# Inverse row sums brought to the features' partitions by one product with a 0/1 matrix of heads, in place of two transposes

## The chip, the core and the metric

The kernel runs on one core of a Trainium2 chip. A core has engines that run side by side, each through its own instructions in order: TensorE (PE, with its weight loads PEld), VectorE (DVE), ScalarE (ACT), GpSimd (POOL) and SyncE (SP), which issues most transfers. They wait for one another through semaphores. On-chip memory has 128 partitions; TensorE writes into PSUM, which the kernel uses in banks. The metric is the device time of one execution in microseconds.

## What is computed

Attention with a hash mask, then a feed-forward network (FFN) over all tokens. Cut to what matters, with 4 batches, 8 heads, 768 positions, head size 64, model width 512 and FFN width 2048:

```python
mask = q_bucket[:, :, :, None] == k_bucket[:, :, None, :]   # 6 sign bits of a projection
scores = np.where(mask, scale * q @ k.T, -1e9)
attn = np.exp(scores - scores.max(-1))
attn = attn / (attn.sum(-1) + 1e-09)
x = (attn @ v) with heads side by side: (3072 tokens, 512)
h = x @ w_in
out = (h * np.clip(h + 3, 0, 6) / 6) @ w_out
```

The division by the row sum belongs to a token and a head. The kernel does not divide the attention matrix. It multiplies the attention's output by 1 / (row sum + 1e-9) just before the FFN reads it.

## The kernel before

**Precision.** Operands of the large matmuls are split into a rounded high part and the rest (type fp32r), and three products, high x high, high x low and low x high, are added in PSUM. Splits are a copy on ACT for the high part and a subtraction on DVE or POOL for the low part.

**Attention.** A step k works on 128 queries of one head; 6 steps make a head and 192 make the whole. `scores` (L405) fills a pair of PSUM banks. `lowest` on DVE (L412) takes the row minimum of the negated scores and copies them to SBUF, and `exponential` on ACT (L424) gives the probabilities, with the row sums as a by-product in `sms[b]`, tokens on partitions: [128, 6, 8 heads]. Then the probabilities are turned so that keys are on partitions. Up to step 101 PE does this with transposes (`transp`, L434); later `flip` on DVE (L445) transposes blocks of 32x32, and `move` sends them through DRAM into the tiles `spare` and `px`. `split_p` (L491 on ACT, L493 on POOL, L495 on DVE) splits them, `values` (L517, L531) multiplies by v, `output` (L567) copies out of PSUM, and SP and POOL (`add`, L542) write the transposed result, unnormalised, to DRAM. Once per head the next head's hash bits are taken: `hash_qk` (L345) on PE and `bits` (L364) on DVE.

**FFN.** Batch 0 is done in the middle of the kernel by `first_ffn`. Batches 1 to 3 are done by the generator `ffn`, in chunks of 256 tokens, three to a batch, nine in all; chunks are named b_t for batch and chunk here. A chunk takes 16 steps, one for each 128 columns of the FFN's width: `gemm1` (L686, 12 matmuls of 256 columns), `gate` (L708 on ACT, L709 on DVE, then L714 on ACT and L715 on DVE for the split) and `gemm2` (L724, L725, L729) for the step before. The FFN generator is advanced by hand inside the attention's steps at the calls `go("A")` to `go("D")`, and the order of PE, DVE, ACT and POOL is written out by hand (`manual_schedule`). From step 101 on this is called paced. After the attention ends, the rest of the FFN runs alone; that stretch is the tail here.

**Normalising a chunk.** `load_x` brings the chunk's features back from DRAM as `xr`, [128 features, 4 groups, 256 tokens]. Features are on partitions, but the inverse row sums have tokens on partitions. `scale_x` lists six things to do, and `begin` puts them into `side`, from which the FFN's loop takes one at a time beside its own work (in paced steps for batches 1 and 2 one per step, in stage D at the step's end; for batch 3 two per step, after some empty entries):

1. `invert`: `inverse` on DVE, one addition (L587) and one reciprocal (L588) of 128x16;
2. `spread_next(0)`: `spread` on POOL (L597) copies the inverse of the group's two heads 64 times each into a tile of 128x256 behind the home in `spare`;
3. to 6., for each group of 128 features: `normalise` turns that tile with two transposes on PE (L607) into the PSUM tile `rt`, DVE multiplies the features by it (L610), and POOL spreads the next group, into the same tile.

The multiplications on DVE are collected in `muls` and issued by `multiply()`: in paced steps after the next exponential, and in held steps after the split of the probabilities. When the last step of a chunk is reached, `split_x` (L675 on ACT, L676 on DVE) splits the next chunk's features; for batch 3 this is done group by group.

Chunk 1_0 is normalised before pacing begins, at steps that are marked `held`. PSUM banks for `rt`, `h`, `z` and `acc` come from `bank`, four in turn.

Of the kernel before, what the change touches and what calls it, by code (L numbers as in the profile page):

```python
# [10 lines left out]
F32 = mybir.dt.float32  # L11
F32R = mybir.dt.float32r
BF16 = mybir.dt.bfloat16
U32 = mybir.dt.uint32
AF = mybir.ActivationFunctionType
ALU = mybir.AluOpType
AX = mybir.AxisListType

P = 128
# [24 lines left out]
def lsh_attention_moe(  # L44
# [10 lines left out]
    nc = tc.nc  # L55
    B, H, D, S = qkT.shape
    D //= 2
    DM, DF = w_in.shape
    KT = S // P
# [4 lines left out]
    TC = 256  # L64
# [4 lines left out]
    cp = ctx.enter_context(tc.tile_pool(name="cp", bufs=1))  # L69
    sp = ctx.enter_context(tc.tile_pool(name="sp", bufs=2))  # L70
# [12 lines left out]
    spare = []  # L83
# [7 lines left out]
    turn = 0  # L91

    def bank(shape, name: str, tag: str | None = None):

        nonlocal turn
        if tag is None:
            tag = ("pt", "pu")[turn % 2]
            turn += 1
        return ps.tile(shape, F32, name=name, tag=tag, bufs=2)

    pair_turn = 0
    ffn_on = False
# [9 lines left out]
    thr = cp.tile([P, 1], F32, name="thr")  # L112
    val = cp.tile([P, 1], F32, name="val")
    three = cp.tile([P, 1], F32, name="three")
    ident = cp.tile([P, P], F32, name="ident")
    make_identity(nc, ident)


# [9 lines left out]
    for r, one, big in ((D, 0, -BIG), (ZK, 1, 1.0)):  # L128
# [3 lines left out]
        nc.vector.memset(val[r : r + 2 * NB], big * (1, -1)[1 - one])  # L132
        nc.vector.memset(val[r : r + NB], big * (1, -1)[one])
    nc.vector.memset(three[:], 3.0)

    raw0 = sp.tile([P, S], F32, name="raw0", tag="raw", bufs=1)[:]
    dma(out=raw0, in_=qkT[0, 0])
# [17 lines left out]
    WC = 512  # L155
# [70 lines left out]
    sms = {}  # L226
# [354 lines left out]
    def inverse(name: str, b: int, ts: slice, ccs: range, rc=None):  # L581

        k = slice(ts.start // P, ts.stop // P)
        hs = slice(ccs.start * P // D, ccs.stop * P // D)
        if rc is None:
            rc = sp.tile([P, KT, H], F32, name=f"rc{name}", tag="rc", bufs=1)[:, : k.stop - k.start]
        nc.vector.tensor_scalar_add(rc[:, :, hs], sms[b][:, k, hs], 1e-9)  # L587
        nc.vector.reciprocal(rc[:, :, hs], rc[:, :, hs])  # L588
        return rc

    def spread(name: str, rc, cc: int, to=None):

        hp2 = P // D
        rb = (spare[0][:, S : S + TC] if to is None else to).rearrange(
            "p (u h d) -> p u h d", u=TC // P, h=hp2
        )
        nc.gpsimd.tensor_copy(  # L597
            rb,
            rc[:, :, cc * hp2 : (cc + 1) * hp2].unsqueeze(3).to_broadcast([P, TC // P, hp2, D]),
        )  # L600
        return rb

    def normalise(name: str, x, rb, tag: str | None = None):

        rt = bank([P, TC], f"rt{name}", tag)
        for u in range(TC // P):
            nc.tensor.transpose(  # L607
                rt[:, u * P : (u + 1) * P], rb[:, u].rearrange("p h d -> p (h d)"), ident[:]
            )
        muls.append(lambda: nc.vector.tensor_mul(x, x, rt[:]))  # L610
        if not paced and not held:
            multiply()

    muls = []
    held = False

    def multiply():
        for f in muls:
            f()
        muls.clear()  # L620
# [3 lines left out]
    def piece():  # L624
        if pieces:
            pieces.pop(0)()

    def load_x(b: int, t: int, ccs: range, xr=None):
        assert not pending(b, range(ccs.start * P // D, ccs.stop * P // D), t)
        ts = slice(t * TC, (t + 1) * TC)  # L630
        if xr is None:
            xr = wide_tile([P, NCC, TC], F32, f"xr{b}_{t}")
        of = xs[b][:, ts].rearrange("(cc p) t -> p cc t", p=P)

        def load(cc: int):
            with tc.issue_after(last.ins):
                dma(out=xr[:, cc], in_=of[:, cc])

        if paced:
            for cc in ccs:  # L640
                pieces.append(lambda cc=cc: load(cc))
            piece()
        else:
            dma(out=xr[:, ccs.start : ccs.stop], in_=of[:, ccs.start : ccs.stop])
        return xr

    def scale_x(b: int, t: int, ccs: range, xr, rc=None):

        name = f"{b}_{t}"
        rbs = {}  # L650

        def invert():
            piece()
            def now():
                rbs["rc"] = rc if rc is not None else inverse(name, b, slice(t * TC, (t + 1) * TC), ccs)

            if held:
                muls.append(now)
            else:
                now()  # L660

        def spread_next(cc: int):
            piece()
            if cc < len(ccs):
                rbs[cc] = spread(name, rbs["rc"], cc)

        def then(cc: int):
            normalise(f"{name}_{cc}", xr[:, cc], rbs.pop(cc), "pt" if ffn_on and b == 0 else None)
            spread_next(cc + 1)

        return [invert, lambda: spread_next(0)] + [lambda cc=cc: then(cc) for cc in ccs]

    def split_x(x, src, engine):
        multiply()
# [117 lines left out]
    def widen(cc: int):  # L792

        hs = slice(cc * P // D, (cc + 1) * P // D)
        nc.scalar.copy(
            over[cc].rearrange("p (k h d) -> p k h d", k=KT, h=P // D),
            rc0[0][:, :, hs].unsqueeze(3).to_broadcast([P, KT, P // D, D]),
        )

    def divide(t: int, cc: int, tag: str | None = None):  # L800
        rb = over[cc][:, t * TC : (t + 1) * TC].rearrange("p (u h d) -> p u h d", u=TC // P, h=P // D)
        normalise(f"0_{t}_{cc}", xr0[t][:, cc], rb, tag)
# [5 lines left out]
    def late_rb():  # L808
        late["rc"] = inverse("late", 0, slice(0, S), range(cc3, NCC), rc0[0])
        x = sp.tile([P, NTC, TC], F32, name="rblate", tag="ga", bufs=1)  # L810
        late["rb"] = [
            spread(f"late{t}", late["rc"][:, 2 * t : 2 * t + 2], cc3, x[:, t]) for t in range(NTC)
        ]
# [49 lines left out]
    def first_ffn(resume):  # L863
        nonlocal ffn_on
        ffn_on = True
        normalise("late0", lt(0), late["rb"][0], "pt")
        split_x(x0[0][cc3], lt(0), nc.vector)
        room12(0)
# [74 lines left out]
        ffn_on = False  # L943
        yield

    first_x = []

    def load_first_x():
        spare.append(sp.tile([P, 2 * WC], F32, name="spare", tag="ob", bufs=1))
        first_x.append(load_x(1, 0, range(cc3)))  # L950

    def ffn():
# [10 lines left out]
        def begin(c: int):  # L963
            b, t = chunks[c]
            xr[c] = load_x(b, t, range(NCC) if c else range(cc3, NCC), None if c else first_x[0])
            todo = scale_x(b, t, range(NCC), xr[c])
            if b < B - 1:
                side.extend(todo + [lambda: None] * (0 if paced else 2))
                if not paced:
                    opening.append(lambda: (place(c), [split(c, cc) for cc in range(NCC)]))  # L970
                return

            side.extend([lambda: None] * (4 if t else 6) + todo[:2])
            for cc in range(NCC):
                side.append(todo[2 + cc])
                side.append(lambda cc=cc: (place(c) if cc == 0 else None, split(c, cc)))
# [161 lines left out]
    with tc.manual_schedule(engines={ET.PE, ET.DVE, ET.Activation, ET.Pool}):  # L1138
# [102 lines left out]
        for k in range(NS + LT + 2):  # L1241
# [4 lines left out]
            i, t = divmod(k, KT)  # L1246
# [4 lines left out]
            if k == GF - 6:  # L1251
                load_first_x()
# [123 lines left out]
```

## Time and profile before

| | |
|---|---|
| median of 3 runs | 962.6 us (962.13 to 962.63) |
| profiled execution, its own time | 964.03 us |
| its span, first to last instruction | 962.2 us |
| granted TensorE clock, mean | 1.000 |
| chunks' inversions (L587), start | 376.8, 440.2, 513.0, 584.9, 658.0, 730.4, 804.5, 850.7, 896.3 us |
| DMA | 152.06 MB, mean 158 GB/s |

The page's second part cuts the span into 40 equal slices of 24 us; each digit is the share in tenths that an engine was busy:

```profile
PE   8999999999999999999999999999999999999997
...
DVE  7999988888559999887878888877878874343422
ACT  7898875665469888667766766666766664333332
POOL 6777744666537766555655555555555442000000
```

The profile lists instructions by line of the kernel and engine. "p<-s" means that tile p is written from tile s. A bracket behind a row gives the time in which the engine stood idle before it, and whose work ended that wait. Idle time matters only on the path that sets the end. PE's matmuls overlap, so the distance between starts, not the duration, says what one costs PE.

### The profile page before, as it was taken

Reading aid. Unit: us, or ns where it says so; the run is one execution under the profiler, and the core shown is the slowest. Engines: PE = TensorE matmul, PEld = TensorE weight load, DVE = VectorE, ACT = ScalarE, POOL = GpSimd, SP = SyncE. Lnnn points to the kernel's source line nnn. Section 1 sums busy time; section 2 is a strip of 40 time slices with the busy share of each in tenths; the row PEclk is TensorE's granted clock in tenths of the full one; section 3 lists DMA queues with packets and bytes.
Section 4 is the critical chain, followed back from the end, with each engine's and each line's share of the span. In section 5 each row is a group of like instructions: output and inputs, shape, how many; then the busy total and the mean of one; then the engine's idle time right before and its main releaser. Section 6 shows DMA issues by size and latency. Waiting matters only on the chain.

```text
span 962.2 us, 19452 instructions
## 1 busy us (share of the span) xinstructions
PE 945.7 (98%) x6308; PEld 871.7 (91%) x6308; DVE 722.0 (75%) x1464; ACT 623.5 (65%) x1422; POOL 473.5 (49%) x584
## 2 busy tenths in 40 slices
PE   8999999999999999999999999999999999999997
PEld 7999988999989999889899999999899899899996
DVE  7999988888559999887878888877878874343422
ACT  7898875665469888667766766666766664333332
POOL 6777744666537766555655555555555442000000
PEclk9999999999999999999999999999999999999999
DMA  4567579100035455688888888788888773101000
GB/s 127 137 157 186 132 226 377 62 2 1 6 117 119 112 134 126 174 254 242 249 252 251 239 245 261 237 252 246 263 244 245 219 220 72 44 1 45 1 22 22
DMA packets 113613, 152.06 MB, mean 158 GB/s; under 512 B 13876, under 2 KB 82612, under 8 KB 113512
## 3 DMA queue, kind: packets, MB, share of 16 engines
q1 hardware_dynamic: 108472, 144.79, 49.1%
q0 software_dynamic: 5040, 6.03, 5.4%
q8 instruction: 50, 0.82, 0.4%
q14 instruction: 51, 0.42, 0.1%
HBM read 77.34 MB, written 54.00 MB: 136 GB/s over the span
## 4 chain that ended last, share of the span: by engine, by line
PE 83%; DVE 9%; issue 2%; ACT 2%; DMA 2%; POOL 1%; SPq 0%; DVEq 0%; ACTq 0%; POOLq 0%
PE h L686 26%; PE s L405 11%; PE po L729 7%; PE po L724 7%; PE po L725 7%; PE acc L517 6%; PE acc L531 6%; PE pt L434 5%; PE z L345 3%; DVE p L412 3%; DVE pl L495 2%; DVE qq L364 1%; PE pos L724 1%; PE pt L729 1%; PE pos L725 1%
## 5 line engine op out<-in xcount | busy, mean ns | idle before, releaser
L424 ACT ACTIVATE p<-p,m 128x768 f32<-128x768 f32 x192 | 180.1, 938 | 114.2 <-DVE p L412 105.6
L412 DVE TENSOR_SCALAR_CACHE_REDUCE p<-s 128x768 f32<-128x768 f32 x192 | 182.5, 951 | 18.1 <-PE pt L434 10.9
L405 PE MATMUL s<-kk,qq 128*128 128x384 f32 (+1 forms) x768 | 168.7, 341 | 1.1 <-DVE qq L364 0.4
L709 DVE SCALAR_TENSOR_TENSOR h<-g,h 128x256 f32<-128x256 f32 x192 | 80.9, 422 | 101.2 <-ACT g L708 98.6
L708 ACT ACTIVATE g<-h,three 128x256 f32<-128x256 f32 x192 | 91.0, 474 | 90.7 <-PE h L686 90.1
L686 PE MATMUL h<-xh,w 128*128 128x256 f32 x1024 | 147.4, 283 | 0.3
L405 PEld LDWEIGHTS s<-kk,qq 128*128 128x128 f32 (+1 forms) x768 | 134.4, 189 | 10.9 <-DVE p L412 1.3
L686 PEld LDWEIGHTS h<-xh,w 128*128 128x128 f32 x1024 | 136.6, 188 | 5.5 <-DVE qq L364 1.3
L445 DVE STREAM_TRANSPOSE p<-p 128x768 f32<-128x768 f32 x90 | 88.1, 978 | 64.4 <-ACT p L424 64.4
L493 POOL TENSOR_TENSOR pl<-spare,ph 128x384 fp32r<-128x384 f32 x45 | 45.8, 1017 | 129.2 <-ACT ph L491 89.2
L495 DVE TENSOR_TENSOR pl<-pt,ph 128x384 fp32r<-128x384 f32 x196 | 100.0, 550 | 4.0 <-ACT ph L491 3.5
L724 PE MATMUL po<-w,gb 128*128 128x512 f32 x250 | 99.0, 396 | 1.0 <-ACT gb L714 1.0
L725 PE MATMUL po<-w,gb 128*128 128x512 f32 x250 | 98.5, 394 | 0.0
L491 ACT CAST ph<-pt 128x384 fp32r<-128x384 f32 x196 | 85.6, 474 | 13.6 <-PE pt L434 11.8
L221 POOL TENSOR_TENSOR w<-wr,w 128x128 fp32r<-128x128 f32 x128 | 71.9, 593 | 45.2 <-ACT w L215 41.9
L434 PE MATMUL pt<-ident,p 128*128 128x128 f32 x612 | 85.8, 274 | 2.4 <-DVE pl L495 1.5
L714 ACT CAST gb<-h 128x256 fp32r<-128x256 f32 x141 | 52.4, 372 | 50.0 <-DVE h L709 29.9
L686 PE MATMUL h<-xl,w 128*128 128x256 f32 x512 | 81.8, 281 | 0.0
L434 PEld LDWEIGHTS pt<-ident,p 128*128 128x128 f32 x612 | 71.8, 140 | 9.7 <-PE pt L434 2.3
L729 PE MATMUL po<-w,gb 128*128 128x512 f32 x250 | 78.5, 395 | 0.1
L323 POOL TENSOR_TENSOR kk<-raw,qq 64x192 fp32r<-64x192 f32 (+1 forms) x73 | 65.4, 919 | 24.2 <-ACT qq L309 20.9
L493 POOL TENSOR_TENSOR pl<-px,ph 128x384 fp32r<-128x384 f32 x45 | 46.6, 1036 | 55.7 <-ACT ph L491 42.2
(153 smaller groups left out, 2049.3 us busy)
## 6 DMA issues: line engine op xcount, KB each, us to landing
fd<-p SPq DMA_DIRECT2D x90, 384.0 KB
spare<-fd SPq DMA_DIRECT2D x180, 96.0 KB
px<-fd SPq DMA_DIRECT2D x180, 96.0 KB
kk<-qq SPq DMA_DIRECT2D x62, 192.0 KB
wr<-in_w_in SPq DMA_DIRECT2D x16, 512.0 KB
wr<-in_w_out SPq DMA_DIRECT2D x16, 512.0 KB
raw<-in_qkT SPq DMA_DIRECT2D x19, 384.0 KB
vr<-in_v SPq DMA_DIRECT2D x32, 192.0 KB
```

The source lines that it names most:

```text
L405: nc.tensor.matmul(s[:, c, :HW], lhsT=q[:, us], rhs=half(k, c), start=n == 0, stop=n == 1)
L412: nc.vector.tensor_scalar(out=pr_[:], in0=s[:, :, :HW], scalar1=CAP, scalar2=None, op0=ALU.min, op1=ALU.min, accum_out=m[:],)
L424: nc.scalar.activation(pr_[:], pr_[:], AF.Exp, bias=m[:], scale=-1.0, accum_out=sms[b][:, t, h : h + 1])
L434: nc.tensor.transpose(pt[:, x], probs[g][0][:, c, x * P : (x + 1) * P], ident[:])
L445: nc.vector.transpose(x, x)
L493: engine.tensor_sub(lo, pt, hi.bitcast(F32))
L495: lows.append(lambda: engine.tensor_sub(lo, pt, hi.bitcast(F32)))
L686: nc.tensor.matmul(hp, lhsT=wi[:, wp, wc], rhs=x[cc][xp], start=(k == 0 and cc == 0), stop=(k == 2 and cc == NCC - 1),)
L708: nc.scalar.activation(r[:], hp, AF.Relu, bias=three[:], scale=1.0)
L724: nc.tensor.matmul(po[u], lhsT=gh[:, us], rhs=wo[:, 0], start=(fc == 0), stop=False)
L725: nc.tensor.matmul(po[u], lhsT=gh[:, us], rhs=wo[:, 1], start=False, stop=False)
L729: nc.tensor.matmul(po[u], lhsT=gl[:, us], rhs=wo[:, 0], start=False, stop=(fc == NFC - 1))
```

## The change

The inverse row sums reach the features' partitions by one rounded matmul per group. Two matrices of zeros and ones are made once at the start, from the identity: `heads`, [128, 8], which is one where a partition's number modulo 8 is the head, and `places`, [128, 8], one where the partition belongs to that sixteenth.

Per chunk, `turn_sums` has two halves. The first, at `invert`, does the addition and reciprocal on DVE as before and then two operations on POOL, which split the inverse into a rounded high part and a low part, 128x16 each, side by side in a tile of 128x32. The second, at the next entry of `side`, runs on DVE: a transpose of 32x32 blocks of that tile, and a product of 128x256 that puts the turned values onto a diagonal pattern, `diag`, behind the home in `spare`.

Per group, POOL widens the group's two columns of `heads` to a 128x128 matrix (`spread_heads`); it no longer depends on the row sums. PE multiplies it by `diag` (`normalise_chunk`): for each feature and token exactly the high and the low part of the right inverse are added. `rt` is then multiplied as before.

The 128x128 matrix takes the place of the identity in memory (tag "ident"), except in chunk 1_0, where the identity is still in use and a tile of tag "ga" is taken. Batch 0 keeps its transposes.

```diff
+    marks = cp.tile([P, 2, H], BF16, name="marks")
+    heads, places = marks[:, 0], marks[:, 1]
+    def mark():
+        x = sp.tile([P, KT, H], F32, name="rcmarks", tag="rc", bufs=1)
+        for y, of in enumerate(("p (x h) -> p h x", "p (h x) -> p h x")):
+            nc.vector.tensor_reduce(
+                out=x[:, y], in_=ident[:].rearrange(of, h=H), axis=mybir.AxisListType.X, op=ALU.add
+            )
+        nc.vector.tensor_copy(marks[:], x[:, :2])
+    mark()
...
+    def turn_sums(name: str, b: int, t: int):
+        n = TC // P
+        x = sp.tile([P, KT, H], F32, name=f"rc{name}", tag="rc", bufs=1)
+        rc = x[:, :n]
+        hl = x[:, n : 3 * n].rearrange("p (u x) h -> p u x h", u=n)
+        turned = x[:, n : 3 * n].rearrange("p x h -> p (x h)")
+        nc.vector.tensor_scalar_add(rc, sms[b][:, n * t : n * t + n], 1e-9)
+        nc.vector.reciprocal(rc, rc)
+        nc.gpsimd.tensor_copy(hl[:, :, 0].bitcast(F32R), rc)
+        nc.gpsimd.tensor_sub(hl[:, :, 1].bitcast(F32R), rc, hl[:, :, 0])
+        yield
+        nc.vector.transpose(out=turned, in_=turned)
+        nc.vector.tensor_mul(
+            diag.rearrange("p (u b c) -> p u b c", u=n, c=32),
+            turned.unsqueeze(1).unsqueeze(1).to_broadcast([P, n, P // 32, 32]),
+            places.rearrange("p (b u) -> p u b", u=n).unsqueeze(3).to_broadcast([P, n, P // 32, 32]),
+        )
+
+    def normalise_chunk(name: str, x, cc: int):
+        rt = bank([P, TC], f"rt{name}")
+        nc.tensor.matmul(rt[:], lhsT=rows.pop(), rhs=diag, start=True, stop=True)
+        times(x, rt)
+
+    def spread_heads(name: str, cc: int):
+        if name == "1_0":
+            w = sp.tile([P, 3, TC], F32R, name=f"rows{name}_{cc}", tag="ga", bufs=1)[:, 0, :P]
+        else:
+            w = cp.tile([P, P], F32R, name=f"rows{name}_{cc}", tag="ident", bufs=1)[:]
+        n = P // D
+        nc.gpsimd.tensor_copy(
+            w.rearrange("p (h d) -> p h d", d=D),
+            heads[:, n * cc : n * cc + n].unsqueeze(2).to_broadcast([P, n, D]),
+        )
+        rows.append(w)
...
         def then(cc: int):
-            normalise(f"{name}_{cc}", xr[:, cc], rbs.pop(cc), "pt" if ffn_on and b == 0 else None)
+            normalise_chunk(f"{name}_{cc}", xr[:, cc], cc)
             spread_next(cc + 1)
...
-        return [invert, lambda: spread_next(0)] + [lambda cc=cc: then(cc) for cc in ccs]
+        def widen():
+            turn()
+            spread_next(0)
+
+        return [invert, widen] + [lambda cc=cc: then(cc) for cc in ccs]
...
-        spare.append(sp.tile([P, 2 * WC], F32, name="spare", tag="ob", bufs=1))
+        x = sp.tile([P, 2 * WC], F32R, name="spare", tag="ob", bufs=1)
+        spare.append(x[:, :S].bitcast(F32))
+        diag = x[:, S : S + TC]
```

More of the change, by code (lines that the diff above doesn't have):

```diff
@@ L114, in lsh_attention_moe @@
     three = cp.tile([P, 1], F32, name="three")
-    ident = cp.tile([P, P], F32, name="ident")
+    ident = cp.tile([P, P], F32, name="ident", tag="ident", bufs=1)
     make_identity(nc, ident)
@@ L589, in inverse, with spread @@
         return rc
-    def spread(name: str, rc, cc: int, to=None):
+    def spread(name: str, rc, cc: int, to):
         hp2 = P // D
-        rb = (spare[0][:, S : S + TC] if to is None else to).rearrange(
-            "p (u h d) -> p u h d", u=TC // P, h=hp2
-        )
+        rb = to.rearrange("p (u h d) -> p u h d", u=TC // P, h=hp2)
         nc.gpsimd.tensor_copy(
@@ L609, in normalise, with times @@
             )
+        times(x, rt)
+    def times(x, rt):
         muls.append(lambda: nc.vector.tensor_mul(x, x, rt[:]))
@@ L612, in normalise @@
             multiply()
+    def turn_sums(name: str, b: int, t: int):
[18 more added lines that the diff above has]
+        nc.tensor.matmul(rt[:], lhsT=rows.pop(), rhs=diag, start=True, stop=True)
+        times(x, rt)
+    rows = []
+    def spread_heads(name: str, cc: int):
[9 more added lines that the diff above has]
+        rows.append(w)
     muls = []
@@ L645, in load_x, with scale_x, turn @@
         return xr
-    def scale_x(b: int, t: int, ccs: range, xr, rc=None):
+    def scale_x(b: int, t: int, ccs: range, xr):
         name = f"{b}_{t}"
-        rbs = {}
         def invert():
             piece()
-            def now():
-                rbs["rc"] = rc if rc is not None else inverse(name, b, slice(t * TC, (t + 1) * TC), ccs)
+            turn()
+        turned = turn_sums(name, b, t)
+        def turn():
+            now = lambda: next(turned, None)
             if held:
@@ L660, in invert, with then @@
                 now()
+        def then(cc: int):
+            normalise_chunk(f"{name}_{cc}", xr[:, cc], cc)
+            spread_next(cc + 1)
         def spread_next(cc: int):
@@ L664, in spread_next @@
             if cc < len(ccs):
-                rbs[cc] = spread(name, rbs["rc"], cc)
-        def then(cc: int):
-            normalise(f"{name}_{cc}", xr[:, cc], rbs.pop(cc), "pt" if ffn_on and b == 0 else None)
-            spread_next(cc + 1)
-        return [invert, lambda: spread_next(0)] + [lambda cc=cc: then(cc) for cc in ccs]
+                spread_heads(name, cc)
+        def widen():
+            turn()
+            spread_next(0)
+        return [invert, widen] + [lambda cc=cc: then(cc) for cc in ccs]
     def split_x(x, src, engine):
@@ L944, in first_ffn @@
         yield
-    first_x = []
+    first_x, diag = [], None
     def load_first_x():
-        spare.append(sp.tile([P, 2 * WC], F32, name="spare", tag="ob", bufs=1))
+        nonlocal diag
+        x = sp.tile([P, 2 * WC], F32R, name="spare", tag="ob", bufs=1)
+        spare.append(x[:, :S].bitcast(F32))
+        diag = x[:, S : S + TC]
         first_x.append(load_x(1, 0, range(cc3)))
```

## The prediction

> **What bounds the kernel now.** First the page: its busy shares, then its chain of work that ended last.
>
> ```profile
> PE 945.7 (98%) x6308; PEld 871.7 (91%) x6308; DVE 722.0 (75%) x1464; ACT 623.5 (65%) x1422; POOL 473.5 (49%) x584
> ...
> PE 83%; DVE 9%; issue 2%; ACT 2%; DMA 2%; POOL 1%; SPq 0%; DVEq 0%; ACTq 0%; POOLq 0%
> ```
>
> PE sets the end for 83% of the span. But DVE stands on the chain too, for 9%, so an edit that moves work from PE to DVE has to be weighed place by place. The view of groups, shapes apart, has what the change touches and the nearest kin of what it adds:
>
> ```profile
> L607 PE MATMUL rt<-ident,spare 128*128 128x128 f32 x72 | 13.8, 273 | 0.0
> L610 DVE TENSOR_TENSOR xr<-xr,rt 128x256 f32<-128x256 f32 x45 | 18.4, 410 | 0.7 <-PE rt L607 0.6
> L597 POOL COPY spare<-rc 128x256 f32<-128x256 f32 x36 | 17.1, 475 | 102.1 <-DVE rc L588 75.9 <-PE rt L607 25.5
> L588 DVE RECIPROCAL rc<-rc 128x16 f32<-128x16 f32 x9 | 2.3, 253 | 0.3
> L587 DVE TENSOR_SCALAR rc<-sms 128x16 f32<-128x16 f32 x9 | 1.9, 211 | 0.1
> L445 DVE STREAM_TRANSPOSE p<-p 128x768 f32<-128x768 f32 x90 | 88.1, 978 | 64.4 <-ACT p L424 64.4
> L676 DVE TENSOR_TENSOR xl<-xr,xh 128x256 fp32r<-128x256 f32 x28 | 10.3, 419 | 2.6 <-ACT xh L675 2.6
> L267 POOL TENSOR_TENSOR pjl<-pjh,pr 64x6 fp32r<-64x6 f32 x2 | 0.4, 195 | 0.0
> ```
>
> There are 72 transposes: two for each of 4 feature groups in 9 chunks, so 36 places. A PE row's 273 ns is latency, as matmuls overlap. What one place costs is read from the distance of starts, in PE's timeline and in the chain of work (both: start, duration, instruction):
>
> ```profile
> 901.57 0.38 PE L607 MATMUL rt<-ident,spare 128*128 128x128 f32 x2
> ...
> 904.59 0.38 PE L607 MATMUL rt<-ident,spare 128*128 128x128 f32 x2
> ...
> 907.62 0.38 PE L607 MATMUL rt<-ident,spare 128*128 128x128 f32 x2
> ```
>
> ```profile
> 938.76 1.41 PE h L686 x12
> 944.36 1.41 PE h L686 x12
> ```
>
> One step with a pair takes 3.01 to 3.03 us. Two steps without take 5.60, or 2.80 each. A pair costs **0.22 us** of PE.
>
> **The change part by part.** *PE.* One product of 256 columns takes the place of the pair. The same shape in the rounded type is h: 12 in 1.41 us, 0.117 us each. Below it cannot be less than one transpose of half its columns, about 0.11; above, I bound it by the pair's 0.22. I take 0.117, the same shape and type: 0.10 us less at each place, 36 x 0.10 = **3.6 us** if PE were the limit at all of them. The Trainium skill, "Perfetto Trace Analysis", section "Transposes", says to do transposes as transposes and not as ordinary matmuls, since these skip the arithmetic. By it the pair would be the cheaper form and the 3.6 would be 0 (a rival, below). The rows of h and of the pair speak against it here: 256 columns at 0.117 us against 2 x 128 at 0.22.
>
> *DVE.* Added for each chunk, one step after the reciprocal: a 32x32 block transpose of 128x32 and a product of 128x256. The transpose lies between the 0.21 us of a 128x16 operation and the 0.98 of 128x768; nearest is the small one, 0.20. The product is nearest to L676, also two SBUF operands, 0.42, of which the next instruction overlaps some 0.07: 0.35. Together **0.55 us**, at the end of a step and ahead of the next row minimum (L412), so the exponential and the flip (L445) behind it move too. Above, a subtraction of 128x384 with both operands in SBUF has taken this long:
>
> ```profile
> 525.43 1.91 DVE L495 TENSOR_TENSOR pl<-px,ph 128x384 fp32r<-128x384 f32 x1
> 525.56 1.28 POOL L493 TENSOR_TENSOR pl<-px,ph 128x384 fp32r<-128x384 f32 x1
> ```
>
> So the product's upper end is 1.9, where POOL works beside it. The Trainium skill, "SBUF — State Buffer", section "SBUF: two separate sides", has a rule for it: a DVE operation with two SBUF inputs and a GpSimd operation that reads SBUF lock each other out for a whole instruction; these two rows agree. By it the insertion could come to the 1.9; I stay at 0.55, since the added pair runs a step after POOL's small operations.
>
> *POOL.* Two operations of 128x16 are added per chunk, between the reciprocal and the transpose: nearest is L267, 0.2 us each (0.1 to 0.48, the large copy). The four copies shrink from 128x256 to 128x128 and no longer wait for the reciprocal, at most 0.2 us less each. POOL is at 49%; I count these at nothing, except where DVE waits for the first two at once. Queued behind a waiting copy stay the subtractions of L493, as before.
>
> *At the start*, two reductions and a copy on DVE, some 0.6 us by L587 and L676:
>
> ```profile
> 1.73 0.06 DVE L133 MEMSET val<- 6x1 f32 x1
> ...
> 3.89 0.56 DVE L296 CAST qq<-raw 64x768 fp32r<-64x768 f32 x1 [2.10 <-DMA raw<-in_qkT]
> ```
>
> DVE idles 2.1 us there for the first input: nothing. If that cover were gone, 0.6.
>
> **Chunk by chunk**, b_t for batch and chunk, rows of the timeline where nothing else is said, against the 964.03 us of the profiled run (span 962.2).
>
> 1_0, not yet paced. Its first product needs the new diagonal tile, written at the end of the half step before it.
>
> ```profile
> 378.05 1.02 DVE L495 TENSOR_TENSOR pl<-pt,ph 128x384 fp32r<-128x384 f32 x2
> ...
> 379.05 0.38 PE L607 MATMUL rt<-ident,spare 128*128 128x128 f32 x2
> ...
> 379.25 0.96 DVE L412 TENSOR_SCALAR_CACHE_REDUCE p<-s 128x768 f32<-128x768 f32 x1 [0.19 <-PE pt L434]
> ```
>
> DVE is free for the added pair at about 379.07 (378.05 + 1.02) and done at 379.6, so PE waits 0.55 and the minimum starts 0.35 later. I let two of the four savings stand: 0.55 - 0.2, **+0.4**.
>
> 1_1, 2_1, 2_2: DVE loses 0.55 and soon meets a wait that another engine or a transfer ends:
>
> ```profile
> 449.69 0.96 DVE L412 TENSOR_SCALAR_CACHE_REDUCE p<-s 128x768 f32<-128x768 f32 x1 [0.88 <-DMA fd<-p]
> ...
> 670.19 0.43 DVE L709 SCALAR_TENSOR_TENSOR h<-g,h 128x256 f32<-128x256 f32 x1 [0.61 <-ACT g L708]
> ...
> 752.42 0.43 DVE L709 SCALAR_TENSOR_TENSOR h<-g,h 128x256 f32<-128x256 f32 x1 [0.86 <-ACT g L708]
> ```
>
> Idle times of 0.88, 0.61 and 0.86 cover it. PE's 0.4 is mostly lost too, since PE in turn waits at these places and where the next chunk's split ends: **0, -0.1, 0**.
>
> 1_2: from its diagonal tile to the next chunk DVE waits for nothing but its own minimum's exponential (the view of waits, us 518 to 541), and PE then waits for DVE's split:
>
> ```profile
> DVE p L445 <- ACT p L424: 2.5, 5, 0.8
> ```
>
> ```profile
> 540.38 1.43 DVE L676 TENSOR_TENSOR xl<-xr,xh 128x256 fp32r<-128x256 f32 x4
> ...
> 541.30 0.95 PE L686 MATMUL h<-xl,w 128*128 128x256 f32 x4
> ```
>
> Four such matmuls start within 0.35 us when nothing holds them; here they take 0.95 with the last's latency of 0.28, so 0.3 of waiting. DVE's 0.55 goes through in full, and the savings end in that wait: **+0.55**.
>
> 2_0: the hash bits come soon after, and PE resumes where they end:
>
> ```profile
> 593.56 1.29 DVE L364 TENSOR_SCALAR qq<-z,thr,val 44x384 fp32r<-44x384 f32 x2
> ```
>
> ```profile
> 594.39 0.41 PE L607 MATMUL rt<-ident,spare 128*128 128x128 f32 x2
> 594.90 1.21 PE L686 MATMUL h<-xh,w 128*128 128x256 f32 x8
> ```
>
> 0.55 later; the three places after it keep 0.3: **+0.25**.
>
> 3_0: here inversion and diagonal tile fall into one step, ahead of a gate's low part.
>
> ```profile
> 804.66 0.25 DVE L588 RECIPROCAL rc<-rc 128x16 f32<-128x16 f32 x1
> ...
> 804.98 0.40 POOL L597 COPY spare<-rc 128x256 f32<-128x256 f32 x1 [3.28 <-DVE rc L588]
> ...
> 805.04 0.42 DVE L715 TENSOR_TENSOR ga<-h,ga 128x256 fp32r<-128x256 f32 x1
> ...
> 805.73 0.62 PE L729 MATMUL po<-w,gb 128*128 128x512 f32 x2
> ```
>
> POOL's two from 804.98 to 805.4, transpose and product to 806.05, the low part to 806.45, and L729 waits for it: 0.7. Four savings against it: **+0.3**.
>
> 3_1 and 3_2, the tail, where only the FFN runs:
>
> ```profile
> 850.91 0.25 DVE L588 RECIPROCAL rc<-rc 128x16 f32<-128x16 f32 x1
> ...
> 851.32 0.40 POOL L597 COPY spare<-rc 128x256 f32<-128x256 f32 x1 [35.31 <-DVE rc L588]
> ...
> 852.30 0.43 DVE L709 SCALAR_TENSOR_TENSOR h<-g,h 128x256 f32<-128x256 f32 x1 [1.14 <-ACT g L708]
> ...
> 853.17 0.42 DVE L715 TENSOR_TENSOR ga<-h,ga 128x256 fp32r<-128x256 f32 x1 [0.44 <-ACT ga L714]
> ...
> 855.48 0.62 PE L729 MATMUL po<-w,ga 128*128 128x512 f32 x2
> ```
>
> POOL to 851.7, DVE's pair to 852.4: 0.1 past an idle stretch, off the path, since the low part behind it ends 1.9 us ahead of its matmul at 855.48. All savings stay: **-0.4 each**.
>
> Sum: 0.4 + 0 + 0.55 + 0.25 - 0.1 + 0 + 0.3 - 0.8 = **+0.6**: 964.6 for a run like the profiled one. That run lies 1.4 above the median of 962.6; on the median's scale, **963.2 us**.
>
> **The rivals.** *PE's saving is kept.* DVE's delay is absorbed in 1_2 and 2_0 as in 1_1, and all five paced chunks keep 0.4. For it: PE's 98%. Against it: the rows at 541 and 594, where DVE ends the wait. 0.4 - 2.0 + 0.3 - 0.8 = -2.1: 960.5. With all 36 kept, 959.0.
>
> *The added DVE pair costs about double*, 1.1 us, because its product is locked out beside POOL (the rows at 525). It decides from about 0.9 on, the idle times that cover it. Six chunks, the first and the five paced, are then 0.55 worse each: 0.6 + 3.3 = +3.9: 966.5, slower. For it, that such long rows exist; against it, POOL's idle 102 us ahead of its copies.
>
> *The product is no cheaper than the pair*, which is what the change wouldn't do of what it says: the losses stay without the savings, 0.5 + 0.55 + 0.55 + 0.7 = +2.3: 964.9. The rows of h speak against it. It is what the Trainium skill's rule on transposes, cited above, would have.
>
> **How the numbers follow.** Forecast 0.60, saving kept 0.20, pair at double 0.14, product no cheaper 0.06. About 0.2% (1.9 us) is what a measurement of this kernel can tell from no change. Within it lies the forecast; faster is the second case; slower are the last two. 963.2 alone would range from 961.3 to 964.6; the range reaches to most of the saving and to the product that is no cheaper: 960.2 to 965.5.
>
> **What would show it.** PE's steps with a product in the tail at 2.91 us instead of 3.02; DVE's added pair at 0.6 us of rows; PE waiting about 0.5 us near 379 and 0.7 near 805; longer waits for DVE at the bits of 2_0 and at the split behind 1_2. The forecast is wrong if DVE's delay is covered there too, or if the pair's rows come out near 1 us.

## The result, and the profile after

The changed kernel takes 968.79 us (median of 6 runs, 968.23 to 969.6), the kernel before 962.71 (6 runs, 962.13 to 963.06): a ratio of 1.0062 [1.0051, 1.0072], **slower by 6.1 us**. The forecast was 963.2, with a range that ended at 965.5. The profiled run of the changed kernel took 968.73, with a span of 967.0; against that of before, 4.7 longer (it lies at its median, that of before 1.3 above). The traces are compared on that scale.

The page of the changed kernel, its busy shares and its chain of work that ended last:

```profile
PE 947.3 (98%) x6272; PEld 871.4 (90%) x6272; DVE 728.3 (75%) x1485; ACT 623.1 (64%) x1422; POOL 471.3 (49%) x602
...
PE 85%; DVE 8%; ACT 2%; issue 2%; DMA 2%; POOL 1%; SPq 0%; DVEq 0%; ACTq 0%; POOLq 0%
```

PE has 36 matmuls fewer and is busy 1.6 us *longer*; on the chain its share rose, and DVE's fell. That does not look like a kernel in which PE was spared 3.6 us and DVE became the limit. PE itself ran longer for less work. Its groups, shapes apart:

```profile
L664 POOL CAST rows<-marks 128x128 fp32r<-128x128 bf16 x36 | 13.7, 380 | 24.3 <-PE rt L652 23.7
L652 PE MATMUL rt<-spare,rows 128*128 128x256 f32 x36 | 10.9, 302 | 1.5 <-DVE spare L643 1.0 <-DVE qq L378 0.5
L643 DVE TENSOR_TENSOR spare<-rc,marks 128x256 fp32r<-128x256 f32 x9 | 4.3, 478 | 0.3
L642 DVE STREAM_TRANSPOSE rc<-rc 128x32 f32<-128x32 f32 x9 | 1.8, 203 | 1.8 <-POOL rc L639 1.8
L639 POOL TENSOR_TENSOR rc<-rc 128x16 fp32r<-128x16 f32 x9 | 2.0, 221 | 0.7
L638 POOL CAST rc<-rc 128x16 fp32r<-128x16 f32 x9 | 1.8, 197 | 78.0 <-DVE rc L637 77.8
```

The added operations cost what was forecast: DVE's transpose 203 ns, POOL's two 197 and 221, and DVE's product 425 in eight chunks. Its mean of 478 comes from one execution of 902, in chunk 1_0. The products wait 1.5 us in all, of which 1.0 for DVE's product and 0.5 for the hash bits: far less than 6.

PE's timeline in the tail shows the saving:

```profile
903.39 0.28 PE L652 MATMUL rt<-spare,rows 128*128 128x256 f32 x1
906.31 0.28 PE L652 MATMUL rt<-spare,rows 128*128 128x256 f32 x1
909.25 0.28 PE L652 MATMUL rt<-spare,rows 128*128 128x256 f32 x1
```

A step with the product takes 2.92 and 2.94 where one with the pair took 3.02 and 3.03: 0.09 to 0.10 saved at each place, as forecast.

So where did the 4.7 of the traces come from? I subtracted the start of each row exponential and each gate in the trace of before from that of the same one after. How far the changed kernel lags, at the borders of each stretch:

| stretch (us of before) | what runs there | lag at its start | at its end | gained or lost | forecast |
|---|---|---|---|---|---|
| 0 to 143 | start, batch 0 | 0 | -0.43 | -0.4 | 0 |
| 143 to 275 | batch 0's FFN, untouched by the diff | -0.43 | 0.49 | **+0.9** | 0 |
| 275 to 371 | batch 1's attention | 0.49 | 0.65 | +0.2 | 0 |
| 371 to 399 | chunk 1_0 | 0.65 | 2.76 | **+2.1** | +0.4 |
| 399 to 786 | the five paced chunks | 2.76 | 5.28 | **+2.5** | +0.7 |
| 787 to the end | 3_0 to 3_2 | 5.27 | 4.74 | -0.5 | -0.5 |

Three stretches lost clearly more than forecast, and one of them isn't touched by the diff. Each got experiments of its own. The clock does not explain it: the granted clock is 1.00 in every trace from 16 us until 3 us before the end.

### The profile page after: what moved, and what is told of

It reads as the page before. It is cut to its first block, busy times and chain, and to the rows that moved or that the text cites. A ratio compares the mean times of both kernels' runs of the same rounds, so it can differ in the third digit from the quotient of the medians.

```text
span 967.0 us, 19397 instructions
## 1 busy us (share of the span) xinstructions
PE 947.3 (98%) x6272; PEld 871.4 (90%) x6272; DVE 728.3 (75%) x1485; ACT 623.1 (64%) x1422; POOL 471.3 (49%) x602
## 4 chain that ended last, share of the span: by engine, by line
PE 85%; DVE 8%; ACT 2%; issue 2%; DMA 2%; POOL 1%; SPq 0%; DVEq 0%; ACTq 0%; POOLq 0%
PE h L748 27%; PE s L419 11%; PE po L791 7%; PE po L786 7%; PE po L787 7%; PE acc L545 6%; PE acc L531 6%; PE pt L448 5%; PE z L359 3%; DVE pl L509 2%; DVE p L426 2%; DVE qq L378 1%; PE pos L786 1%; PE pos L787 1%; PE pt L787 1%
## 5 line engine op out<-in xcount | busy, mean ns | idle before, releaser
L426 DVE TENSOR_SCALAR_CACHE_REDUCE p<-s 128x768 f32<-128x768 f32 x192 | 182.4, 950 | 19.3 <-PE pt L448 11.0
L505 ACT CAST ph<-pt 128x384 fp32r<-128x384 f32 x196 | 85.7, 473 | 14.9 <-PE pt L448 11.9
```

The lines of the kernel that those rows point to most:

```text
L426: nc.vector.tensor_scalar(out=pr_[:], in0=s[:, :, :HW], scalar1=CAP, scalar2=None, op0=ALU.min, op1=ALU.min, accum_out=m[:],)
```

## The experiments

The theories at the start: **DVE's pair** of transpose and product is late for PE, in 1_0 and in the paced chunks; **place**: the new small tiles move all later tiles in SBUF by 32 bytes and more, and this slows code that the diff doesn't touch; against both, **the product itself** is dearer than the pair wherever PE is not in the tail. Results, each as a ratio to the kernel before run beside it:

| kernel | median us (runs) | before | ratio, 95% interval |
|---|---|---|---|
| pad32 | 963.13 (11) | 962.84 | 1.0003 [0.9994, 1.0012] |
| pad32sp | 963.53 (11) | 962.84 | 1.0006 [0.9998, 1.0015] |
| aligned | 966.63 (5) | 962.84 | 1.0041 [1.0027, 1.0054] |
| aligned_first_old | 964.37 (11) | 962.84 | 1.0019 [1.0010, 1.0027] |
| placed | 967.2 (5) | 962.71 | 1.0043 [1.0030, 1.0056] |
| once | 962.2 (11) | 962.71 | 0.9995 [0.9986, 1.0004] |
| twice | 966.14 (5) | 962.71 | 1.0039 [1.0026, 1.0051] |
| hidden | 961.36 (11) | 962.71 | 0.9986 [0.9977, 0.9995] |
| late_first | 965.09 (11) | 963.23 | 1.0015 [1.0006, 1.0024] |
| sp192 | 964.74 (11) | 963.23 | 1.0018 [1.0009, 1.0027] |
| after_hidden | 967.0 (5) | 963.23 | 1.0038 [1.0025, 1.0050] |
| hidden_all | 962.59 (11) | 963.55 | 0.9991 [0.9982, 1.0001] |

Differences between two of these kernels are taken between their ratios, times 962.7.

### The place of tiles in memory

**pad32** is the kernel before with an unused tile of 32 bytes behind the identity, so that all later tiles lie 32 bytes further on.

```diff
     make_identity(nc, ident)
+    pad = cp.tile([P, 16], BF16, name="pad")
+    nc.vector.memset(pad[:], 0.0)
```

> The kernel before with one unused tile of 32 bytes per partition behind the identity, so that every later tile lies 32 bytes further on; nothing else is changed. Theory A (place in memory): in the profile of the changed kernel the low FFN operand's matmuls start 118 to 120 ns apart instead of 117 also in stretches that the change does not touch (batch 0's FFN loses 0.9 us), because the new small tiles move the large ones by an odd multiple of 32 bytes; then this kernel is 1.5 to 3.5 us slower than the kernel before (964.2 to 966.2). Theory B (the change's own work alone costs the 6 us): no difference, within 0.5 us of 962.7.

**pad32sp** has that tile at the head of the second pool, so that PE's operands move against the weights.

```diff
+    pad = sp.tile([P, 16], BF16, name="pad", tag="pad", bufs=1)
+    nc.vector.memset(pad[:], 0.0)
     raw0 = sp.tile([P, S], F32, name="raw0", tag="raw", bufs=1)[:]
```

> As the kernel with 32 bytes more behind the identity, but the unused tile stands ahead of the second pool, so that the FFN's weights stay where they were and the operands (features, probabilities, keys, queries) move by 32 bytes. Theory A with the moving operands as the cause: 1.5 to 3.5 us slower. Theory A with the weights' tiles as the cause: within 0.5 us of 962.7. Theory B: within 0.5 us of 962.7.

Neither differs from before by more than its interval: 32 bytes alone cost nothing that can be measured. The trace of pad32 also shows how much a single execution drifts: it ends 1.9 us ahead of that of before, 1.0 of that gained between 399 and 456 us, with the same instructions. So a loss in one stretch of one trace is known to within 1 to 2 us at best, and what a kernel costs as a whole is taken from the medians.

**aligned** is the changed kernel with its two rows of marks in unused bytes of two old small tiles, and the scratch of the start in the tag of another tile, so that the large tiles lie where they lay before (or a multiple of 1024 bytes off).

```diff
-    thr = cp.tile([P, 1], F32, name="thr")
-    val = cp.tile([P, 1], F32, name="val")
+    thr = cp.tile([P, 8], F32, name="thr")
+    val = cp.tile([P, 8], F32, name="val")
+    heads, places = (x[:, 4:].bitcast(BF16) for x in (thr, val))
+    thr, val = thr[:, :1], val[:, :1]
...
-    marks = cp.tile([P, 2, H], BF16, name="marks")
-    heads, places = marks[:, 0], marks[:, 1]
...
-        x = sp.tile([P, KT, H], F32, name="rcmarks", tag="rc", bufs=1)
+        x = sp.tile([P, TC], F32, name="rcmarks", tag="g", bufs=1)[:, : 2 * H].rearrange("p (y h) -> p y h", h=H)
...
-        nc.vector.tensor_copy(marks[:], x[:, :2])
+        nc.vector.tensor_copy(heads, x[:, 0])
+        nc.vector.tensor_copy(places, x[:, 1])
```

> The changed kernel with the two matrices of heads and places kept in unused bytes of the small constant tiles and the scratch for making them in another tile, so that all large tiles lie where they lay before, up to a multiple of 1024 bytes. The computation is the same. Theory A: 2 to 3.5 us faster than the changed kernel, 965.3 to 966.8, and batch 0's FFN as long as in the kernel before. Theory B: 968.8 as the changed kernel, within 0.7.

1.0041 against the changed kernel's 1.0062: 2.0 us less, though the intervals touch. Batch 0's FFN then lost nothing (a lag of -0.41 at its start, -0.43 at its end).

**placed** is the other way round: the kernel *before*, with unused tiles that put every tile at the address it has in the changed kernel (32 bytes on in the first pool, 224 in the second).

```diff
+    pad = cp.tile([P, 16], BF16, name="pad")
+    nc.vector.memset(pad[:], 0.0)
+    first = sp.tile([P, KT, H], F32, name="first", tag="rc", bufs=1)
+    nc.vector.memset(first[:], 0.0)
     raw0 = sp.tile([P, S], F32, name="raw0", tag="raw", bufs=1)[:]
```

> The kernel before, with nothing but unused small tiles that put every later tile at exactly the address that it has in the changed kernel. Theory A in its narrower form (the distance between operands and weights in memory, not their parity alone, sets the matmuls' pace; moving all tiles by 32 bytes, or one pool by 32, made no difference, but going back to the old places gave 2.2 us): 1.5 to 3 us slower than the kernel before, 964.3 to 965.8, with the low FFN operand's matmuls of batch 0 1.5 ns further apart. Rival (the 2.2 us came from other things that the kernel with the old places differs in): within 0.7 us of 962.8.

1.0043: the unchanged program is 4.1 us slower when its tiles lie elsewhere, more than the 1.5 to 3 expected. **sp192** keeps only the second of the two tiles, 192 bytes, ahead of the second pool.

```diff
+    first = sp.tile([P, KT, H], F32, name="first", tag="rc", bufs=1)
+    nc.vector.memset(first[:], 0.0)
     raw0 = sp.tile([P, S], F32, name="raw0", tag="raw", bufs=1)[:]
```

> The kernel before with the second pool's tiles 192 bytes further on (an unused tile of the size of the inverses stands first) and the weights' pool where it was. Theory A': the distance of 192 bytes between operands and weights, which the changed kernel has besides the 32 bytes on both, is the cause: batch 0's FFN loses 0.9 us as in the kernel with all of the changed places, and the whole 2 to 4.5 us. Rival (the weights' 32 bytes are needed too, or only the total counts): less than 1 us slower.

1.0018, or 1.7 us, which the interval separates from none, but less than the 2 expected at least. What is slow is seen in the chain of work in batch 0's FFN (start, us, the piece), where PE waits for nothing. Before, then the changed kernel, then aligned, then sp192:

```profile
202.10 1.41 PE h L686 x12
```

```profile
202.04 1.44 PE h L748 x12
...
204.88 1.42 PE h L748 x12
```

```profile
201.68 1.41 PE h L748 x12
```

```profile
202.07 1.44 PE h L688 x12
...
204.91 1.42 PE h L688 x12
```

The same twelve matmuls of 256 columns take 1.41 us in before and in aligned, 1.42 to 1.44 in the changed kernel and in sp192. Counted over the traces, as the mean distance from the start of such a matmul to the start of PE's next one, in ns ("after" is the changed kernel; distances of 260 ns and more are left out):

| matmuls | before | pad32 | pad32sp | aligned | after | placed | sp192 |
|---|---|---|---|---|---|---|---|
| h, fed by px, batch 0 | 118.5 | 118.4 | 117.8 | 118.4 | 121.2 | 121.2 | 121.2 |
| h, fed by xl, batch 0 | 116.8 | 116.8 | 117.9 | 116.6 | 118.3 | 118.3 | 118.2 |
| h, fed by xl, 400 to 800 us | 117.6 | 117.5 | 118.7 | 117.6 | 120.3 | 120.3 | 120.2 |

Placed and sp192, both the old program, have the changed kernel's slow pace to a tenth of a nanosecond, and what the three share is that the second pool lies 192 bytes further from the first (in after and placed 224 less 32). Pad32 and pad32sp both have the second pool 32 bytes further on; the pace changes only in pad32sp, where the first pool stays behind, and there one row gets faster and two get slower. The pace of h is thus shown to be a matter of place, and of the place of one pool against the other. It is enough for sp192's 1.7 us, and in batch 0's FFN it costs the same 0.9 us in after, placed and sp192. It does not account for all of placed's 4.1: by its trace 0.8 arose ahead of the first h, and 1.2 between 532 and 570 us, where sp192 with the same pace of h lost 0.7. Why stays open.

### Chunk 1_0

**aligned_first_old** is aligned with the old transposes in chunk 1_0 alone.

```diff
+        if name == "1_0":
+            nc.vector.tensor_scalar_add(rc, sms[b][:, n * t : n * t + n], 1e-9)
+            nc.vector.reciprocal(rc, rc)
+            rbs["rc"] = rc
+            return
...
+        if cc in rbs:
+            normalise(name, x, rbs.pop(cc))
+            return
...
+            to = sp.tile([P, 3, TC], F32, name=f"rb{name}_{cc}", tag="ga", bufs=1)[:, 0]
+            rbs[cc] = spread(name, rbs["rc"], cc, to)
+            return
```

> As the kernel with the old places in memory, but chunk 1_0 is normalised in the old way, with two transposes per group. Theory C (chunk 1_0, where PE stands 1.05 us before its first product because the diagonal tile is made at the end of the half step before, costs 2.1 us by the traces): 1.7 to 2.3 us faster than the kernel with the old places. Rival (that delay is made good later, as in the paced chunks): no more than 0.5 us faster.

1.0019 against 1.0041, 2.1 us less; in the traces the stretch from 371 to 399 us went from +2.1 to -0.2. What happens there, in the changed kernel's timeline:

```profile
379.46 0.59 POOL L664 CAST rows<-marks 128x128 fp32r<-128x128 bf16 x1
...
379.63 0.20 DVE L642 STREAM_TRANSPOSE rc<-rc 128x32 f32<-128x32 f32 x1
...
379.69 0.80 POOL L393 CAST vv<-vr 128x384 fp32r<-128x384 f32 x1
...
379.87 0.90 DVE L643 TENSOR_TENSOR spare<-rc,marks 128x256 fp32r<-128x256 f32 x1
...
380.70 0.94 DVE L426 TENSOR_SCALAR_CACHE_REDUCE p<-s 128x768 f32<-128x768 f32 x1
...
380.92 0.36 PE L652 MATMUL rt<-spare,rows 128*128 128x256 f32 x1 [1.05 <-DVE spare L643]
```

DVE's product takes 0.90 in place of 0.42 while POOL copies, and PE stands for 1.05 us behind it. The row minimum, L426, starts 1.07 after the transpose, and the exponential, the split and the next scores come after it. Which of the two counts, PE's wait or the late minimum? **late_first** is aligned with one empty step between the diagonal tile and its first product, so the same DVE work stands at the same place and PE's wait goes.

```diff
-        return [invert, widen] + [lambda cc=cc: then(cc) for cc in ccs]
+        idle = [lambda: None] * (name == "1_0")
+        return [invert, widen] + idle + [lambda cc=cc: then(cc) for cc in ccs]
...
-                side.extend(todo + [lambda: None] * (0 if paced else 2))
+                side.extend(todo + [lambda: None] * (0 if paced else 1))
```

> The kernel with the old places and the product in all nine chunks; in chunk 1_0 the first product is taken one step later than its diagonal tile, with an empty entry between. Theory E (what chunk 1_0 costs is PE's wait of 1.06 us for a tile that is made too late): 0.8 to 1.5 us faster than with the old places alone (966.6). Rival (the cost is DVE's 1.1 us of added pair in a stretch where every step ends on DVE, wherever it stands): within 0.5 us of 966.6.

1.0015 against aligned's 1.0041: 2.5 us less, as much as putting the old transposes back. Its timeline:

```profile
378.87 0.91 DVE L643 TENSOR_TENSOR spare<-rc,val 128x256 fp32r<-128x256 f32 x1
...
379.70 0.94 DVE L426 TENSOR_SCALAR_CACHE_REDUCE p<-s 128x768 f32<-128x768 f32 x1
...
382.88 0.28 PE L652 MATMUL rt<-spare,rows 128*128 128x256 f32 x1
```

The product is as slow as ever and the minimum as late, but PE's first product, 3 us later, waits for nothing, and in the traces the stretch lost only 0.24 us. So DVE's late minimum alone is not what cost.

But PE's wait is only half of the 2.1 either, which is why late_first gained more than the 0.8 to 1.5 expected. In the changed kernel the lag rises by 1.14 us at that wait, and by another 0.93 at 399 us, where a row minimum waits for a transfer of probabilities to DRAM. First before, where no such wait stands, then the changed kernel:

```profile
395.11 0.97 SPq L78 DMA_DIRECT2D fd<-p  x1
396.17 1.16 SPq L78 DMA_DIRECT2D raw<-in_qkT  x2
```

```profile
396.48 1.01 SPq L78 DMA_DIRECT2D raw<-in_qkT  x1
397.59 0.54 SPq L78 DMA_DIRECT2D fd<-p  x1
...
401.00 0.96 DVE L426 TENSOR_SCALAR_CACHE_REDUCE p<-s 128x768 f32<-128x768 f32 x1 [1.00 <-DMA fd<-p]
```

SP issues an input ahead of the first `fd<-p`. Its order is not among those written by hand. The changed kernel, aligned and after_hidden have it this way round and wait 1.0 to 1.2 us; the other kernels issue `fd<-p` first and have no such wait. Aligned_first_old and late_first thus took away two things, PE's wait and this order. No run has one without the other, so whether the wait brought the order about, and what each is worth alone, stays open.

### DVE's pair in the paced chunks

With place and 1_0 out of the way, aligned_first_old still lost 1.7 us between 399 and 786 us of its trace, though PE's 20 products there should save 2.0. Two kernels vary only DVE's work; SP's order is the same in aligned_first_old, in both of them and in hidden below. **once** makes the diagonal tile for chunk 1_1 alone; the later chunks use that one again, so this leaves out part of the computation.

```diff
+        if name != "1_1":
+            return
         nc.vector.transpose(out=turned, in_=turned)
```

> The kernel with the old places and with transposes in chunk 1_0, in which the block transpose and the diagonal product are made for chunk 1_1 alone; the later chunks are multiplied with that chunk's inverses, so this leaves part of the computation out. Theory D (DVE's added pair is what costs in the paced chunks, where its 0.6 us goes through to PE): 2 to 3 us faster than the same kernel with all pairs (964.4), 961.4 to 962.4, so 0.5 to 1.5 faster than the kernel before. Rival (PE's saving is swallowed by other waits and the pair is hidden): within 0.7 us of 964.4.

**twice** writes the diagonal tile twice over in the eight chunks that have one.

```diff
+        if name != "1_0":
+            nc.vector.tensor_mul(
+                diag.rearrange("p (u b c) -> p u b c", u=n, c=32),
...
         nc.vector.tensor_mul(
```

> The kernel with the old places and with transposes in chunk 1_0, in which the diagonal product of 128x256 is made twice in the other eight chunks, 0.37 us more of DVE each. Theory D: five paced chunks pass on most of it, 1.0 to 2.0 us slower than 964.4. Rival (hidden): no more than 0.5 us slower.

Both move the time: from 1.0019 to 0.9995 (2.3 us less) without seven of the pairs, and to 1.0039 (1.9 us more) with a second product in eight chunks. The product on PE is the same in all three, so the third theory falls. Seven pairs fewer are worth 0.33 each, eight products more cost 0.24 each. By the traces most of it arises in the paced chunks, which lost 1.7 in aligned_first_old, gained 0.5 in once and lost 2.8 in twice; the tail gained 1.0, 1.5 and 0.7.

**hidden** leaves the work in, and moves the pair in the paced chunks. It is queued ahead of the flip that waits for the next exponential, in place of ahead of the row minimum. (Chunk 3_0 still counts as paced here, so its pair moves too, behind the gate's low part; the tail gained 1.1 in hidden's trace against 1.0 without that.)

```diff
             now = lambda: next(turned, None)
-            if held:
+            if held or paced and rows_late:
                 muls.append(now)
...
         def widen():
+            nonlocal rows_late
+            rows_late = True
             turn()
+            rows_late = False
+            late_turn.append(1)
             spread_next(0)
...
+        if late_turn:
+            late_turn.clear()
+            if not held:
+                multiply()
```

> The kernel with the old places and with transposes in chunk 1_0, in which the block transpose and the diagonal product of a paced chunk are issued one step later, behind the exponential and ahead of the flip, where DVE stands idle for 0.76 us in a step without a multiplication. Theory D: the pair costs nothing there, 961.3 to 962.4, as without the pairs. Rival (the pair is not the cost): within 0.7 us of 964.4.

DVE's timeline in chunk 1_2, in before (the same flip, no pair), in aligned_first_old and in hidden:

```profile
520.14 0.98 DVE L445 STREAM_TRANSPOSE p<-p 128x768 f32<-128x768 f32 x1 [0.76 <-ACT p L424]
```

```profile
517.01 0.20 DVE L647 STREAM_TRANSPOSE rc<-rc 128x32 f32<-128x32 f32 x1
...
517.25 0.42 DVE L648 TENSOR_TENSOR spare<-rc,val 128x256 fp32r<-128x256 f32 x1
...
517.59 0.95 DVE L426 TENSOR_SCALAR_CACHE_REDUCE p<-s 128x768 f32<-128x768 f32 x1
...
519.64 0.98 DVE L459 STREAM_TRANSPOSE p<-p 128x768 f32<-128x768 f32 x1 [0.76 <-ACT p L438]
```

```profile
518.43 0.20 DVE L647 STREAM_TRANSPOSE rc<-rc 128x32 f32<-128x32 f32 x1
518.65 0.42 DVE L648 TENSOR_TENSOR spare<-rc,val 128x256 fp32r<-128x256 f32 x1
519.26 0.98 DVE L459 STREAM_TRANSPOSE p<-p 128x768 f32<-128x768 f32 x1 [0.18 <-ACT p L438]
```

The bracket is the reading to take along. DVE idles 0.76 us ahead of the flip in before already, since the flip needs ACT's exponential and that needs the minimum. A pair ahead of the minimum leaves this idle time as long as it was: minimum, exponential and flip all move together. In hidden the pair, 0.6 us, stands *in* the idle time, only 0.18 of it is left, and the flip starts 0.38 earlier than in aligned_first_old, though this trace came into the chunk 0.2 later. The result is 0.9986 [0.9977, 0.9995]: 3.2 us less than aligned_first_old, and **faster than both kernels**, 0.14% below the one before.

The two traces set against each other say where the 3.2 arose. Aligned_first_old falls behind hidden by 0.64 us in 1_1, 0.58 in 1_2, 0.58 in 2_0, 0.61 in 2_1 and 0.80 in 2_2 (lags at 444 and 460, 512 and 528, 588 and 600, 660 and 688, 736 and 760 us), 3.2 together: about the pair's own time in every chunk.

Against the trace of before the paced chunks now gain 1.9, about the 2.0 that 20 places at 0.10 should give. But that trace lies 1.3 above its median, and by the medians hidden is only 1.35 us faster in all, of which the tail's 12 places have about 1.1. How much of the 2.0 the paced chunks keep is therefore not shown. The view of waits, PE's alone, 399 to 786 us (what it waited for: us in total, times, longest) shows a part of it; a wait of 0.2 for POOL, the same in all three, is left off. Before, aligned_first_old, hidden:

```profile
PE po L724 <- ACT gb L714: 1.0, 2, 0.5
PE z L345 <- ACT y L567: 0.2, 1, 0.2
```

```profile
PE po L798 <- ACT gb L788: 1.0, 2, 0.5
PE acc L545 <- ACT ph L505: 0.6, 1, 0.6
PE rt L660 <- DVE qq L378: 0.6, 1, 0.6
PE h L760 <- DVE qq L378: 0.5, 3, 0.2
```

```profile
PE po L808 <- ACT gb L798: 1.0, 2, 0.5
PE h L770 <- DVE qq L378: 0.5, 3, 0.2
PE acc L545 <- ACT ph L505: 0.4, 1, 0.4
```

The new waits, 1.7 us in all, are for the hash bits, L378, and for the high part of the split, L505, on DVE and ACT; hidden loses 0.8 of them. None of them names the pair, L648. The rest of the difference stands in no row of this view.

### Together

**after_hidden** is the changed kernel with only the pair moved, so old places and 1_0's wait are as in the change.

```diff
-            if held:
+            if held or paced and rows_late:
```

> The changed kernel, places and chunk 1_0 as they are, with nothing but the paced chunks' block transpose and diagonal product moved behind the exponential. Theory D: 2 to 3.5 us faster than the changed kernel (968.8), as from 964.4 to 961.4 with the old places. Rival (in the changed places PE is slow enough that DVE's pair is hidden anyway): within 0.7 us of 968.8.

1.0038 against 1.0062: 2.3 us less, where the move alone had given 3.2.

**hidden_all** is late_first with the pair moved: products in all nine chunks, no wait in 1_0, the old places.

```diff
-            if held:
+            if held or paced and rows_late:
...
+        idle = [lambda: None] * (name == "1_0")
```

> The product in all nine chunks with the old places, the paced chunks' pair behind the exponential, and in chunk 1_0 the first product one step after its diagonal tile. Theory E and D together: the four savings of chunk 1_0 come on top, 960.6 to 961.4 against 961.4 with transposes there. Rival (the pair in chunk 1_0 costs more than four savings even without PE's wait, as the two kernels at 965.1 and 964.4 let one think): 961.7 to 962.3.

0.9991 [0.9982, 1.0001]: the rival's figure, and not better than hidden, which keeps the old transposes in 1_0. Four more products there bring nothing that can be measured.

## Why the prediction was wrong, point by point

**The product on PE, 0.10 us less at each place: right.** The tail's steps of 2.92 to 2.94 show it; how much of it the paced chunks of hidden keep is not shown. The rival by the Trainium skill, "Perfetto Trace Analysis", section "Transposes", that the product would be no cheaper than the pair, fails on these rows, for a product of half the instructions in the rounded type.

**DVE's pair, 0.55 in place: right in size in eight chunks of nine** (0.20 and 0.425; in the rows of aligned_first_old the minimum starts 0.58 after the transpose). In the ninth, 1_0, it was 0.20 and 0.90.

**1_0, +0.4: wrong.** The step that failed is "done at 379.6, so PE waits 0.55". PE waited 1.05, as the product took 0.90 beside POOL's copies L664 and L393. I had quoted the row of 1.91 us and the Trainium skill's rule in "SBUF — State Buffer", "SBUF: two separate sides", and set them aside because the pair runs a step after POOL's small operations. That is so, but POOL's large copies stand there. The mechanism of that rival was real in this one chunk; its price for all six was not. The rule fits (0.90 beside POOL, 0.425 without), but no run here took POOL's copies away from that place. The stretch then lost 2.1 and not 1.05: 1.14 came at this wait, and 0.93 at 399 us, where SP issued `fd<-p` behind an input and the row minimum waited for it. The prediction had no term for SP's order. late_first got both back.

**1_1, 2_1, 2_2 at 0, 1_2 at +0.55, 2_0 at +0.25: the sum was wrong, 0.7 forecast and 1.7 measured in aligned_first_old.** The step that failed is "idle times of 0.88, 0.61 and 0.86 cover it". These idle times lie on DVE, but the work pushed back is a row minimum, and behind it come ACT's exponential, the flip and the split that PE needs; DVE's own idle time for a gate or a transfer does not bring these forward. once, twice and hidden show that it is the pair's place, and set against hidden the pair was covered in no chunk: 0.64, 0.61 and 0.80 in the three that were to cover it, 0.58 each in 1_2 and 2_0. For these two the mechanism was right: in the changed kernel PE's product waits 0.49 for the hash bits in 2_0 (0.05 in hidden), and savings end in the wait for the split behind 1_2, where the four matmuls fed by xl take 1.27 in place of 0.95 (1.23 in hidden, so this wait stays when the pair is moved).

**3_0, +0.3 by a stall of 0.7 at L729: wrong.** No stall came; the changed kernel's timeline:

```profile
810.62 0.21 DVE L642 STREAM_TRANSPOSE rc<-rc 128x32 f32<-128x32 f32 x1 [0.60 <-POOL rc L639]
...
810.82 0.63 PE L791 MATMUL po<-w,gb 128*128 128x512 f32 x2
...
810.87 0.43 DVE L643 TENSOR_TENSOR spare<-rc,marks 128x256 fp32r<-128x256 f32 x1
...
811.21 0.42 DVE L777 TENSOR_TENSOR ga<-h,ga 128x256 fp32r<-128x256 f32 x1
```

DVE is late as forecast (it waited 0.60 for POOL, and the low part L777 ended at 811.63). But that low part goes into *ga*, and the matmul right behind it reads *gb*. The row that I quoted said so by its operand; I took the nearest consumer for the right one. The tail as a whole came out at the -0.5 that I forecast, but by luck, as two errors cancel: no stall, and in the changed kernel less of the saving than in aligned_first_old, where it gained 1.0.

**The start, nothing: right.** DVE's reductions end at 2.6 us in the changed kernel's timeline and the first input comes at 3.95.

```profile
1.70 0.58 DVE L143 TENSOR_REDUCE rcmarks<-ident 128x8 f32<-128x128 f32 x2
...
3.95 0.56 DVE L310 CAST qq<-raw 64x768 fp32r<-64x768 f32 x1 [1.35 <-DMA raw<-in_qkT]
```

**The place of tiles: not in the sum at all.** The diff allocates a tile of 32 bytes ahead of the weights and takes the 192-byte scratch earlier; I counted their instructions and not their bytes: 2.0 us by aligned, 1.7 by sp192, up to 4.1 by placed. Place alone did not put the time outside the range: aligned, at 1.0041, would be 966.6, still above 965.5; only with 1_0 gone too (aligned_first_old, 964.5) is the time inside. Place, 1_0 and the pair, at 2.0 + 2.1 + 3.2 us by the steps from the changed kernel over aligned and aligned_first_old to hidden, are together 7.3 (1.0062 to 0.9986). That splits the whole, but each part is known only to within 1 to 2 us, and the parts depend on the order: moved alone, the pair was worth 2.3, and place alone 4.1.

## What to carry to other kernels

When work moves from a busy engine to a less busy one, ask which instruction it is put ahead of, and follow that one's consumers back to the busy engine; idle time on the receiving engine is a cover only if the work is queued inside it, behind the instruction that the others wait for. Put at least a step between making an operand and the first matmul that reads it, and read the operand's name before calling a consumer late. And a new small tile is also a change of address for all tiles behind it, and a moved instruction can change the order of a queue that the program leaves open: compare both before reading a few microseconds as the work of the diff.

## What was not expected of the hardware

PE's pace depended on where operands and weights lie relative to each other: 192 bytes between the two pools took the h matmuls from 118.5 to 121.2 ns (fed by px) and from 116.8 to 118.2 (fed by xl), at a granted clock of 1.00 in batch 0's FFN in before and after alike; 32 bytes on all tiles changed no pace; on the second pool alone they took px from 118.5 to 117.8 and xl from 116.8 to 117.9, with no measurable cost in all. With the 192 bytes an unchanged program was 1.7 us slower, and 4.1 at the changed kernel's exact addresses. Which distances are slow, and why, was not tried.
